# Causal masks by 64-column matmuls, and a stationary padded from 16 to 128 columns

## The chip, the cores and the metric

The kernel runs on one core of one Trainium2 chip. The metric is the device time of one execution in microseconds (us), as the median of the runs shown. Where a profile is read, times are those of one profiled execution.

## The reference, cut to what matters

Two layers, each an attention block and a gated MLP block, on 2048 rows of 640 numbers. Only the attention concerns us. It has 32 heads of 20 columns, and the rows are cut into four segments of 512, inside which each row sees itself and the rows before it:

```python
H = 32; Dh = D // H; N = 4; L = S // N          # D = 640, S = 2048, so L = 512
mask = (ar[:, None] < ar[None, :]) * (-1e9)     # ar = arange(L)
for s in range(N):
    logits = einsum("bhqd,bhkd->bhqk", qs, ks) * scale + mask
    p = softmax(logits, axis=-1)
    a_dot = einsum("bhqk,bhkd->bhqd", p, vs)
    ...                                          # a memory of the segments before, mixed in by a gate
```

## The kernel before, in words

Each layer runs three phases: `phase1a` (attention, class `Attention`), `phase1b` (attention's output matmul for the last rows, layer norm, the MLP's first matmul) and `phase2` (the spatial matmul and the MLP's last matmul). The change touches `phase1a` and the constants built at the start.

**Pairs and steps.** Attention goes through 64 pairs of heads per layer, 4 segments by 16 pairs. The two heads of a pair lie on partitions 0 to 63 and 64 to 127 of one tile `qk`, so that their matmuls use the upper and the lower 64 rows of the array: two instructions with 64 rows each, one per head, follow each other and run side by side. A pair takes three steps c = 0, 1, 2 of `scores` (line 791). A step computes, for pair n, blocks of the transposed logits into the PSUM tile `es` (keys on the partitions, line 816), and for pair n+2 blocks of the logits into the PSUM tile `mp` (queries on the partitions, line 816 too). Steps 0 and 2 have one block of each kind; step 1 has two of each. A block is 128 partitions by 128 to 512 columns, and its one square of 128 by 128 on the diagonal has to be masked.

**The masks.** `mask` (line 781) is called for each block, each head h and each half s = 0, 1: it adds a large negative number above the diagonal by a matmul that accumulates on the block (line 788). The stationary is `big`, 64 rows by 128 columns, with 60000 on a diagonal that picks the 64 output partitions of half s; the moving operand is `maskq` or `maskk`, which holds -60000 where the mask is to be. The 64 partitions of one half need the mask on 64 columns, those of the other half on all 128, so that two of the four mask matmuls of a block (two heads by two halves) have 64 columns and two have 128. In `es` the half s = 0 is the narrow one, in `mp` the half s = 1. The order on PE is: half 0 of all blocks (`es`, then `mp`), then half 1 of all blocks.

**What follows a step.** ScalarE (ACT) takes exp of `es` into `P` (line 825), VectorE (DVE) reduces `mp` to row maxima `mx` (line 832). Both PSUM tiles exist once, so the next step's blocks wait for these readers. After step 2, DVE splits the maxima, scaled and negated, into two f16 parts, `mh`, 128 rows by 16 columns (lines 836, 837). `maxes` (line 851) turns them on PE by a matmul with `mh` as the stationary and an identity of 128 columns as the moving operand, into `mtp` (line 856); ACT copies the 16 rows to `mr` (line 858), and two DMAs from SyncE's queue (SP) put them into rows of `qk` (line 861), from which the maxima enter the logits of `es` two pairs later. `cast` makes f16 high and low parts of `P` on ACT and GpSimd (POOL, lines 847, 848), `pvs` multiplies them with the values on PE (line 875), and `combine` scales and adds on DVE and POOL.

**Fill.** Between the steps PE works on what the next heads and rows need: projections to values, queries and keys (lines 605, 665), the output projection of earlier rows (line 637), the memory (lines 723, 750 to 752).

**What sets the order.** In `phase1a` PE's order is written by hand (`run`, line 910, a list of jobs with due times, under `manual_schedule(engines={PE})`). The order on ACT, DVE, POOL and SP is made when the program is built, by a scheduler that estimates times of all instructions, PE's too. Work with a high priority may be pulled ahead: the first two tiles of `phase1b` (line 316) are loaded and normalized (lines 259, 209, 211, 218) while attention still runs.

Of the kernel before, what the change touches and what calls it, by code (L numbers as in the profile page):

```python
# [8 lines left out]
F32 = mybir.dt.float32  # L9
F32R = mybir.dt.float32r  # L10
F16 = mybir.dt.float16
# [3 lines left out]
ALU = mybir.AluOpType  # L15
# [60 lines left out]
class Weight:  # L76


    def __init__(self, g, nm, c, dram, c0, cols):
        self.g, self.nm, self.c, self.dram, self.c0, self.cols = g, nm, c, dram, c0, cols  # L80
        self.nk = (dram.shape[0] + 127) // 128
        self.kept = [g.nc.dram_tensor(f"w_{nm}{p}", (128, self.nk, cols), F16, kind="Internal").ap() for p in "hl"]
        self.made = False
# [380 lines left out]
def attn_consts(g, cp, beta):  # L464
    nc, tc = g.nc, g.tc

    g.big = cp.tile([128, 192], F16, name="big")
    g.mask = {nm: cp.tile([128, 128], F16, name="mask" + nm) for nm in "qk"}  # L470
    with tc.tile_pool(name="tmp", bufs=1) as tp, tc.tile_pool(name="acp", bufs=1, space=PSUM) as pp:
        f = tp.tile([128, 192], F32, name="fmask")
        for t, n, b, sg, op in ((g.big, 192, -64, 1, ALU.not_equal), (g.mask["q"], 128, 0, -1, ALU.is_ge), (g.mask["k"], 128, -64, 1, ALU.is_ge)):
            nc.vector.memset(f, 0.0)
            for h in range(2):
                v = f[64 * h:64 * h + 64, :n]
                nc.gpsimd.affine_select(v, v, [[sg, n]], op, BIG if op is ALU.not_equal else -BIG, base=b, channel_multiplier=-sg)
            nc.vector.tensor_copy(t, f[:, :n])

        g.gate = cp.tile([128, H], F32, name="gate")  # L480
        g.iomg = cp.tile([128, H], F32, name="iomg")
        nc.sync.dma_start(g.gate, beta.rearrange("(o h) -> o h", o=1).to_broadcast((128, H)))
        nc.scalar.activation(g.iomg, g.gate, AF.Exp)
        nc.vector.tensor_scalar(g.iomg, g.iomg, 1.0, None, ALU.add)
        nc.scalar.activation(g.gate, g.gate, AF.Exp, scale=-1.0)
        nc.vector.tensor_scalar(g.gate, g.gate, 1.0, None, ALU.add)


        row = tp.tile([1, 3, 128], F32, name="mrow")
        nc.vector.memset(row, 0.0)  # L490
        for h in range(2):
            nc.vector.memset(row[:, 0, 64 * h + 62:64 * h + 63], 1.0)
            nc.vector.memset(row[:, 1, 64 * h + 63:64 * h + 64], 1.0)
            nc.vector.memset(row[:, 2, 64 * h + 60:64 * h + 64], MS)
        g.keep = cp.tile([128, 3], F32, name="keep")
        g.qrow = cp.tile([128, 1], F32, name="qrow")
        g.qrow16 = cp.tile([128, 1], F16, name="qrow16")
        kp = pp.tile([128, 4], F32, name="kp")
        for i in range(3):
            nc.tensor.matmul(kp[:, i:i + 1], row[:, i, :], g.ident[0:1, 0:1], start=True, stop=True)  # L500
        nc.vector.tensor_copy(g.keep, kp[:, 0:3])

    g.bmask = cp.tile([128, NU, 8], F32, name="bmask")
    nc.gpsimd.memset(g.bmask, 1.0)
    for m in range(NU):
        n, b = len(TH[m]), 128 * m - DH * TH[m][0]
        v = g.bmask[:, m, :n]
        nc.gpsimd.affine_select(v, v, [[-DH, n]], ALU.is_ge, 0.0, base=b, channel_multiplier=1)
        nc.gpsimd.affine_select(v, v, [[DH, n]], ALU.is_ge, 0.0, base=DH - 1 - b, channel_multiplier=-1)
# [5 lines left out]
class Attention:  # L515
# [9 lines left out]
    def __init__(self, g, x, o_d, x1_d):  # L525
        self.g, self.nc, self.tc = g, g.nc, g.tc
        self.x, self.o_d, self.x1_d = x, o_d, x1_d
        self.st = g.st
        self.gm, self.ot = {}, {}
        self.phq = {}  # L530
        self.P, self.Pf, self.mx, self.mh = {}, {}, {}, {}
        self.pv, self.o = {}, {}
        self.mem, self.last, self.stacked = None, -1, -1
        self.now, self.later, self.rd = None, {}, set()
# [11 lines left out]
    def setup(self, ctx):  # L546
        g, nc, tc = self.g, self.nc, self.tc
        pool = lambda n, b, **k: ctx.enter_context(tc.tile_pool(name=n, bufs=b, reuse_waits="tile", **k))
        sk, self.p3, self.pl2 = pool("ak", 1), pool("a3", 2), pool("al2", 2)
        av, self.u4, self.u2, self.u1 = pool("av", 1), pool("au4", 4), pool("au2", 2), pool("au1", 1)  # L550
        self.e2, self.e1, ax = pool("ae2", 2), pool("ae1", 1), [pool(f"ax{i}", 1) for i in range(2)]
        self.pl1, self.bg = pool("al1", 1), pool("abg", 2)
        self.pd = pool("apd", 2, space=PSUM)
        self.px = pool("apx", 1, space=PSUM)
        self.pm = pool("apm", 1, space=PSUM)
        self.pe = pool("ape", 1, space=PSUM)
        self.po = pool("apo", 1, space=PSUM)
        self.qk = [sk.tile([128, 2, L], F16, name=f"qk{i}") for i in range(self.NQK)]
        self.vs = [p.tile([128, 4, H, 2 * DH + 1], F16, name=f"vs{i}") for i, p in enumerate((av, sk))]
        for t in self.vs:  # L560
            nc.gpsimd.memset(t[:, :, :, DH:DH + 1], 1.0)
        self.xt = [p.tile([128, 2, KD, L], F16, name=f"xt{i}") for i, p in enumerate(ax)]
        self.mst = [self.u1.tile([128, NU, 8, DH + 1], F32, name=f"mst{i}") for i in range(2)]

    def start(self):
# [215 lines left out]
    def mask(self, out, nm, h, o, s):  # L781

        g, nc = self.g, self.nc
        r = slice(64 * h, 64 * h + 64)

        c = slice(64 * s, 128) if nm == "q" else slice(0, 64 * s + 64)
        m = slice(0, 128 - 64 * s) if nm == "q" else slice(64 - 64 * s, 128)
        nc.tensor.matmul(out[:, o + c.start:o + c.stop], g.big[r, 64 - 64 * s:192 - 64 * s], g.mask[nm][r, m], start=False,  # L788
                         stop=s == 1, skip_group_check=True)

    def scores(self, n, c):

        g, nc = self.g, self.nc
        todo = []
        if 0 <= n < self.N:
            q, k = self.qk[n % self.NQK][:, 0], self.qk[n % self.NQK][:, 1]
# [6 lines left out]
        m = n + self.LM  # L803
# [9 lines left out]
        for out, o, w, a, nr, ac, b, bc, _, _ in todo:  # L813
            for h in range(2):
                r = slice(64 * h, 64 * h + nr)
# [12 lines left out]
        if 0 <= m < self.N:  # L828
            if c == 0:
                self.mx[m] = self.pl2.tile([128, 2, 4], F32, tag="mx", name="mx")  # L830
            for i, o, w in red:
                nc.vector.tensor_reduce(self.mx[m][:, :, i], mp[:, :, o:o + w], AX.X, ALU.max)  # L832
            if c == 2:
                mx = self.mx[m]
                mh = self.mh[m] = self.pl2.tile([128, 2, 2, 4], F16, tag="mh", name="mh")
                nc.vector.tensor_scalar(mh[:, :, 0], mx, -1.0 / MS, None, ALU.mult)
                nc.vector.scalar_tensor_tensor(mh[:, :, 1], mx, -1.0 / MS, mh[:, :, 0], ALU.mult, ALU.subtract)

# [12 lines left out]
    def maxes(self, n):  # L851

        g, nc = self.g, self.nc
        del self.mx[n]
        tp = self.pm.tile([128, 512], F32, tag="ms", name="mtp")[:16, :128]
        nc.tensor.matmul(tp, self.mh.pop(n).rearrange("p h i t -> p (h i t)"), g.ident16, start=True, stop=True)
        mr = self.pl2.tile([16, 128], F16, tag="mr", name="mr")
        nc.scalar.copy(mr, tp)
        for h in range(2):
            r = 64 * h + 60  # L860
            nc.sync.dma_start(self.qk[n % self.NQK][r:r + 2, 0].rearrange("i (t c) -> i t c", t=4), mr[8 * h:8 * h + 8])
# [192 lines left out]
def interleaved_layers(ctx, tc, x, wq, wk, wv, wo, beta, w_in, w_sp, b_sp, w_out, out):  # L1054
    nc = tc.nc
    g = Ctx()
    g.nc, g.tc = nc, tc
    cp = consts(g, ctx)
    attn_consts(g, cp, beta)
    prologue(g, ctx, wv, wq, wk, wo, w_in, w_out)  # L1060

# [50 lines left out]
```

## Time and profile before

| | before |
|---|---|
| time, median of 3 runs (lowest to highest) | 2532.6 us (2525.33 to 2532.61) |
| span of the profiled execution | 2529.2 us |
| PE busy in it | 2270.2 us (90%), 21706 matmuls |
| DVE, ACT, POOL busy | 1525.9, 1139.9, 939.6 us |
| masks, line 788 | 4096 matmuls, 98.2 to 1938.5 us |
| turns of the maxima, line 856 | 128 matmuls, 109.7 to 1927.0 us |

The three times are of unprofiled runs. The profiled execution has its span alone, from its first instruction to its last; with whatever lies around the span it stands within the range of the runs, 3.4 us under their median at most.

Attention fills about 100 to 720 us (first layer) and 1338 to 1945 us (second layer) of the span; in between and behind lie the phases without masks. In rows of the timeline the columns are start, duration, engine, line, operation, the program's names, the stationary's and moving operand's shapes ("64\*128 64x64" is a stationary of 64 rows and 128 columns with 64 moving columns on 64 rows), and the number of instructions merged into the row. Matmuls overlap: their durations reach to the end of the array's pipeline, so the pace of a row of matmuls is read from the distance of starts, not from durations. PEld is the loading of the stationary.

### The profile page before, as it was taken

The numbers are of one execution on the slowest core, as the hardware profiler recorded it, in microseconds if no ns is written. First come the engines' busy times: TensorE is split into PE (matmuls) and PEld (weight loads), VectorE is DVE, ScalarE is ACT, GpSimd is POOL, SyncE is SP. The second block draws the span as 40 slices with busy tenths as digits, with TensorE's granted clock in tenths as the row PEclk, the third lists the DMA queues.
The fourth block names the chain that finished last, engine by engine and source line by source line (L and its number), as shares of the span: only waits on it lengthen the run. The fifth ranks groups of instructions, "written<-read, shape, count | busy, mean of one in ns | idle before, by whom it ended". The sixth has DMA issues, their size and how long they took to land. (4 is left out here: it accounts for less than half of the span.)

```text
span 2529.2 us, 52414 instructions
## 1 busy us (share of the span) xinstructions
PE 2270.2 (90%) x21706; PEld 1358.8 (54%) x21706; DVE 1525.9 (60%) x2925; ACT 1139.9 (45%) x1388; POOL 939.6 (37%) x711
## 2 busy tenths in 40 slices
PE   4678788899989998999988889889998999999998
PEld 2345455565655554555554456546565555555555
DVE  6678877777755454544335787787775544444431
ACT  4267766677643231221114677767775332111110
POOL 7066666677631000000042677667775110000000
PEclk9899999899999999999999899989999999999999
DMA  4733644423563478766643244342336335777652
GB/s 141 203 96 101 161 112 112 102 67 105 122 185 94 100 224 217 170 163 156 156 88 91 78 114 97 95 112 70 92 111 167 105 91 143 187 188 174 147 140 64
DMA packets 504575, 325.11 MB, mean 129 GB/s; under 512 B 410576, under 2 KB 445520, under 8 KB 499216
## 3 DMA queue, kind: packets, MB, share of 16 engines
q1 hardware_dynamic: 504336, 321.77, 49.9%
q8 instruction: 169, 2.77, 0.5%
q14 instruction: 70, 0.57, 0.1%
HBM read 148.26 MB, written 85.34 MB: 92 GB/s over the span
## 5 line engine op out<-in xcount | busy, mean ns | idle before, releaser
L848 POOL TENSOR_TENSOR PL<-P,PH 128x1280 f16<-128x1280 f32 x248 | 649.2, 2620 | 319.7 <-ACT PH L847 276.4
L832 DVE TENSOR_REDUCE mx<-mp 128x2 f32<-128x1024 f32 (+3 forms) x512 | 408.8, 820 | 136.8 <-PE mp L788 136.2
L825 ACT ACTIVATE P<-es,sc 128x1024 f32<-128x1024 f32 (+1 forms) x384 | 371.5, 967 | 231.5 <-PE mp L788 184.5
L381 PE MATMUL gp<-zh,wt 128*128 128x432 f16 x2048 | 464.1, 347 | 11.6 <-DMA wt<-wn 11.5
L381 PEld LDWEIGHTS <-wt 128*128 128x128 f16 x3072 | 300.7, 98 | 271.0 <-DMA wt<-wn 12.9
L847 ACT CAST PH<-P 128x1280 f16<-128x1280 f32 x256 | 321.2, 1255 | 8.9 <-PE pv L875 1.4
L300 PEld LDWEIGHTS <-th 128*128 128x128 f16 x1920 | 187.7, 98 | 168.7 <-DMA th<-xnhl 4.1
L381 PE MATMUL gp<-zl,wt 128*128 128x432 f16 x1024 | 271.1, 347 | 0.0
L396 POOL MEMSET un<- 128x64 f16 x32 | 4.8, 151 | 682.1 <-DMA ut<-un 630.8
L816 PEld LDWEIGHTS <-qk 64*128 64x128 f16 (+1 forms) x2048 | 81.6, 96 | 280.5 <-issue 204.9
L212 POOL TENSOR_TENSOR lnrs<-lnve,mhalf 128x1 f32<-128x1 f32 x96 | 58.2, 615 | 440.7 <-DVE lnve L211 433.2
L358 DVE TENSOR_REDUCE am<-wr 128x1 f32<-128x2048 f32 x32 | 73.2, 2286 | 213.1 <-DMA wr<-in_B_w_sp_dram 213.1
L816 PE MATMUL es<-qk 64*128 64x512 f16 (+3 forms) x1024 | 143.1, 313 | 60.2 <-ACT P L825 43.8
L384 ACT ACTIVATE u<-gp,bsp,un 128x864 f32<-128x864 f32 x32 | 34.2, 1068 | 354.8 <-PE gp L381 354.8
L605 PE MATMUL vps<-wvh,xt 128*128 128x320 f16 x640 | 162.5, 324 | 26.5 <-DVE phk L693 8.2
L816 PE MATMUL mp<-qk 60*128 60x512 f16 (+3 forms) x1024 | 141.7, 311 | 47.2 <-DVE mx L832 46.5
L410 PE MATMUL cyp<-wuh,ut 128*128 128x320 f16 (+1 forms) x896 | 164.5, 300 | 11.0 <-DMA ut<-un 10.1
L410 PEld LDWEIGHTS <-ut 128*128 128x128 f16 (+1 forms) x1344 | 131.5, 98 | 67.1 <-DMA ut<-un 12.9
L875 PE MATMUL pv<-vs,PH 128*128 128x41 f16 x2560 | 167.6, 183 | 0.0
L875 PE MATMUL pv<-vs,PL 128*128 128x41 f16 x2560 | 163.9, 181 | 1.6 <-POOL PL L848 1.6
L788 PEld LDWEIGHTS <-big 64*128 64x128 f16 x4096 | 139.1, 97 | 40.7 <-issue 4.7
L368 ACT ACTIVATE wn<-wr,ivw 128x1024 f16<-128x1024 f32 x64 | 71.9, 1143 | 185.5 <-DVE ivw L363 95.3
(186 smaller groups left out, 4331.7 us busy)
## 6 DMA issues: line engine op xcount, KB each, us to landing
wr<-in_B_w_sp_dram SPq DMA_DIRECT2D x32, 1024.0 KB
qk<-st SPq DMA_DIRECT2D x256, 120.0 KB
z<-z SPq DMA_DIRECT2D x32, 432.0 KB
cz<-z SPq DMA_DIRECT2D x32, 432.0 KB
xt<-in_A_x_dram SPq DMA_DIRECT2D x32, 320.0 KB
st<-qhl SPq DMA_DIRECT2D x40, 256.0 KB
st<-khl SPq DMA_DIRECT2D x40, 256.0 KB
x<-x SPq DMA_DIRECT2D x32, 320.0 KB
```

The lines of the kernel that those rows point to most:

```text
L300: nc.tensor.matmul(zp[:, n, :FHH], a[:, k, :], b[:, k, c:c + FHH], start=(k == 0 and j == 0), stop=(k == KD - 1 and j == 2))
L358: nc.vector.tensor_reduce(am, wr, AX.X, ALU.max, apply_absolute_value=True)
L381: nc.tensor.matmul(gp[:, n, :FHH], wt[:, k // 8, a, k % 8, :], b[:, k, n * FHH:(n + 1) * FHH], start=(k == 0 and j == 0), stop=(k == NT - ...
L410: nc.tensor.matmul(yp[:, n, :320], a[:kn[k], k, :], b[:kn[k], k, n * 320:(n + 1) * 320], start=(k == 0 and j == 0), stop=(k == KO - 1 and ...
L605: nc.tensor.matmul(ps, a[:, k, c], b[:, k, n * 320:(n + 1) * 320], start=(i == 0), stop=(i == 14))
L788: nc.tensor.matmul(out[:, o + c.start:o + c.stop], g.big[r, 64 - 64 * s:192 - 64 * s], g.mask[nm][r, m], start=False, stop=s == 1, skip_gr ...
L816: nc.tensor.matmul(out[:, h, o:o + w], a[r, ac], b[r, bc], start=o == 0, stop=False, skip_group_check=True)
L825: nc.scalar.activation(P[:, :, 512 * c:512 * c + ew], es[:, :, :ew], AF.Exp, scale=g.esc)
L832: nc.vector.tensor_reduce(self.mx[m][:, :, i], mp[:, :, o:o + w], AX.X, ALU.max)
L847: nc.scalar.copy(PH, P[:, h])
L848: (nc.gpsimd if h == 0 or n < self.N - self.TAIL else nc.vector).tensor_tensor(PL, P[:, h], PH, ALU.subtract)
L875: nc.tensor.matmul(pv[:, i, h, :], x[:, c:c + 128], v[:, j, h0 + h, :], start=(j == 0 and x is PH), stop=(j == i and x is PL), skip_group_ ...
```

## The change

The roles of the two mask operands are exchanged. The pattern of steps becomes the stationary (`stepq` and `stepk`, 192 columns wide, of which 128 are taken, shifted by 64 for the half), and the diagonal of 60000 becomes the moving operand (`eye`, 64 columns). A matmul now covers all 128 partitions of a strip of 64 columns, where before it covered 64 partitions and up to 128 columns. All four mask matmuls of a block have 64 columns. The number of matmuls, their order and their rows stay.

The stationary `mh` of the turn becomes the first 16 columns of one of two lasting tiles `mhs` of 128 columns, whose other columns are set to zero once per layer. The turn's matmul then writes 128 rows of PSUM instead of 16, of which ACT copies the same 16.

```diff
-    g.big = cp.tile([128, 192], F16, name="big")
-    g.mask = {nm: cp.tile([128, 128], F16, name="mask" + nm) for nm in "qk"}
+    g.eye = cp.tile([128, 64], F16, name="eye")
+    g.step = {nm: cp.tile([128, 192], F16, name="step" + nm) for nm in "qk"}
...
-        for t, n, b, sg, op in ((g.big, 192, -64, 1, ALU.not_equal), (g.mask["q"], 128, 0, -1, ALU.is_ge), (g.mask["k"], 128, -64, 1, ALU.is_ge)):
+        for t, n, b, sg, op in ((g.eye, 64, 0, 1, ALU.not_equal), (g.step["q"], 192, -64, 1, ALU.is_ge), (g.step["k"], 192, 64, -1, ALU.is_ge)):
...
+        self.mhs = [sk.tile([128, 128], F16, name=f"mhs{i}") for i in range(2)]
+        for t in self.mhs:
+            nc.gpsimd.memset(t, 0.0)
...
-        c = slice(64 * s, 128) if nm == "q" else slice(0, 64 * s + 64)
-        m = slice(0, 128 - 64 * s) if nm == "q" else slice(64 - 64 * s, 128)
-        nc.tensor.matmul(out[:, o + c.start:o + c.stop], g.big[r, 64 - 64 * s:192 - 64 * s], g.mask[nm][r, m], start=False,
-                         stop=s == 1, skip_group_check=True)
+        c = o + 64 * s
+        nc.tensor.matmul(out[:, c:c + 64], g.step[nm][r, 64 - 64 * s:192 - 64 * s], g.eye[r], start=False, stop=s == 1,
+                         skip_group_check=True)
...
-                mh = self.mh[m] = self.pl2.tile([128, 2, 2, 4], F16, tag="mh", name="mh")
+                mh = self.mhs[m % 2][:, :16].rearrange("p (h i t) -> p h i t", h=2, i=2)
...
-        tp = self.pm.tile([128, 512], F32, tag="ms", name="mtp")[:16, :128]
-        nc.tensor.matmul(tp, self.mh.pop(n).rearrange("p h i t -> p (h i t)"), g.ident16, start=True, stop=True)
+        tp = self.pm.tile([128, 512], F32, tag="ms", name="mtp")[:, :128]
+        nc.tensor.matmul(tp, self.mhs[n % 2], g.ident16, start=True, stop=True)
...
-        nc.scalar.copy(mr, tp)
+        nc.scalar.copy(mr, tp[:16])
```

PE's order is the same before and after, instruction for instruction; what changes there is operands and widths. On PE, in a step with one block of each kind, the program before has, from the second mask matmul of `es` to the first of its half 1 (`big` is the stationary, a row LDWEIGHTS loads it, the two numbers are the size of what is written):

```order
L788 LDWEIGHTS big
L788 MATMUL es<-maskk,big 128x64
L788 LDWEIGHTS big
L788 MATMUL mp<-maskq,big 128x128
L788 LDWEIGHTS big
L788 MATMUL mp<-maskq,big 128x128
L788 LDWEIGHTS big
L788 MATMUL es<-maskk,big 128x128
```

The same place on PE in the program after (two lines of code are added above the masks in sum, so that line 788 is now 790):

```order
L790 LDWEIGHTS stepk
L790 MATMUL es<-eye,stepk 128x64
L790 LDWEIGHTS stepq
L790 MATMUL mp<-eye,stepq 128x64
L790 LDWEIGHTS stepq
L790 MATMUL mp<-eye,stepq 128x64
L790 LDWEIGHTS stepk
L790 MATMUL es<-eye,stepk 128x64
```

The matmuls stand where they stood; each writes 64 columns, and the stationary differs between `es` and `mp`.

The other engines' order is made anew by the scheduler, which has other estimates for PE. ACT's order is nearly the same; on DVE and SP most rows keep their place or move by a few, and the largest move is that of the first two tiles of `phase1b`. Their statistics (line 209, from the tile `x`, with a number to tell the buffers apart) stand on DVE, before the change, late in attention, at the pairs of the last segment:

```order
L832 TENSOR_REDUCE mx<-mp 128x2
L209 BN_STATS lnst<-x_11881 128x6 x2
L836 TENSOR_SCALAR mh<-mx 128x2x4
L209 BN_STATS lnst<-x_11894 128x6 x2
L210 BN_AGGR lnmv<-lnst 128x2
L837 SCALAR_TENSOR_TENSOR mh<-mx,mh 128x2x4
```

On DVE after the change they stand some 130 instructions earlier, behind the last pair of an earlier segment (`x_11821` and `x_11834` are the same two tiles):

```order
L888 TENSOR_TENSOR rs<-pv,iomg 128x8
L889 RECIPROCAL rs<-rs 128x8
L893 TENSOR_TENSOR ab<-pv,rs 128x328
L209 BN_STATS lnst<-x_11821 128x6 x2
L834 TENSOR_REDUCE mx<-mp 128x2 x2
L209 BN_STATS lnst<-x_11834 128x6
L210 BN_AGGR lnmv<-lnst 128x2
```

The statistics moved ahead past many reductions of `mp`; on SP the two loads of these tiles (line 259) moved ahead by some 70 DMAs with them. The same happens in the second layer.

More of the change, by code (lines that the diff above doesn't have):

```diff
@@ L530, in __init__ @@
         self.phq = {}
-        self.P, self.Pf, self.mx, self.mh = {}, {}, {}, {}
+        self.P, self.Pf, self.mx = {}, {}, {}
         self.pv, self.o = {}, {}
```

## The prediction

> **What bounds the kernel now.** I read first the busy shares, then two stretches of attention (columns: stretch, length, busy time of PE, PEld, DVE, ACT, POOL with counts, granted clock, DMA share, GB/s).
>
> ```profile
> PE 2270.2 (90%) x21706; PEld 1358.8 (54%) x21706; DVE 1525.9 (60%) x2925; ACT 1139.9 (45%) x1388; POOL 939.6 (37%) x711
> ```
>
> ```profile
> 260.00:360.00 100.00, 79.78 (x1073) 52.02 (x1074) 79.61 (x154) 69.87 (x94) 59.70 (x41) 0.93 0.59 149
> 560.00:660.00 100.00, 92.69 (x1359) 58.50 (x1358) 76.82 (x145) 72.55 (x86) 75.18 (x50) 0.95 0.35 96
> ```
>
> The change acts in attention alone, some 1225 us of the span. There PE is the busiest engine late in a layer (92.69 of 100) and level with DVE early (79.78 against 79.61), and the other three work three quarters of the time. So PE leads, but not by much. Next, the waits of PE by releaser (total, times, longest):
>
> ```profile
> PE mp L816 <- DVE mx L832: 46.5, 43, 2.9
> PE es L816 <- ACT P L825: 43.8, 66, 3.6
> PE mtp L856 <- DVE mh L837: 42.9, 22, 6.8
> PE es L816 <- DMA qk<-mr: 13.8, 9, 3.6
> ```
>
> PE waits some 147 us, in 140 pieces of about 1 us. The first two are loops: masks finish `mp` or `es`, the reader empties it, PE may write the next block. A shorter mask lets the reader start sooner, so a gain there passes through the loop if the reader was idle. Last, the chain of waits through the second layer's attention, 1345 to 1945 us:
>
> ```profile
> by line: issue 7.7%; PE kps L665 6.5%; PE qps L665 6.0%; PE pv L875 6.0%; PE es L816 5.3%; PE vps L605 4.8%; ACT P L825 4.7%; DVE mx L832 4.6%; ACT PH L847 4.3%; PE mp L816 4.1%; POOL PL L848 4.0%; PE yps L637 3.3%; PE num L723 2.3%; DMA xt
> ```
>
> PE's entries and "issue" that stand here sum to 46% (7.7 + 6.5 + 6.0 + 6.0 + 5.3 + 4.8 + 4.1 + 3.3 + 2.3). The masks are not among the thirteen, so `es` and `mp` masks have at most 2.3% each, 27.6 us of 600 together.
>
> **The masks.** The pace is read from starts. A step with two blocks of each kind (four instructions per row, two pairs of heads):
>
> ```profile
> 408.07 0.22 PE L788 MATMUL es<-maskk,big 64*128 64x64 f16 x4
> 408.13 0.27 PE L788 MATMUL mp<-maskq,big 64*128 64x128 f16 x4
> 408.24 0.28 PE L788 MATMUL es<-maskk,big 64*128 64x128 f16 x4
> 408.35 0.22 PE L788 MATMUL mp<-maskq,big 64*128 64x64 f16 x4
> 408.51 0.31 PE L637 MATMUL yps<-woh,o 128*128 128x320 f16 x1
> ```
>
> Two pairs of 64 columns take 0.06 us (408.13 − 408.07), two of 128 take 0.11 (408.24 − 408.13, and again 408.35 − 408.24): 0.030 and 0.055 us a pair, so 0.025 saved for each pair that becomes narrow. The last row of masks, 0.16 to the next matmul, is narrow before and after and keeps its price. How many there are:
>
> ```profile
> L788 PE MATMUL es<-maskk,big 64*128 64x128 f16 x1024 | 96.3, 222 | 0.0
> L788 PE MATMUL mp<-maskq,big 64*128 64x128 f16 x1024 | 95.7, 221 | 0.0
> ```
>
> 2048 wide matmuls are 1024 pairs: 1024 × 0.025 = 25.6 us of PE time. Nothing is added: as many matmuls and loads as before, and a stationary of the same 64 rows and 128 columns.
>
> **The turn of the maxima.** With and without the turn between the same neighbours:
>
> ```profile
> 406.03 0.18 PE L875 MATMUL pv<-vs,PL 128*128 128x41 f16 x1
> 406.14 0.22 PE L856 MATMUL mtp<-ident,mh 128*16 128x128 f16 x1
> 406.29 0.31 PE L637 MATMUL yps<-woh,o 128*128 128x320 f16 x1
> ...
> 411.71 0.18 PE L875 MATMUL pv<-vs,PH 128*128 128x41 f16 x1
> 411.73 0.18 PE L875 MATMUL pv<-vs,PL 128*128 128x41 f16 x1
> 411.76 0.30 PE L637 MATMUL yps<-woh,o 128*128 128x320 f16 x1
> ```
>
> Without it `yps` starts 0.03 us after the last `pv`; with it 0.26 (406.29 − 406.03). The 128 columns of the turn are worth 0.055 by the mask pair. So 0.26 − 0.03 − 0.055 = 0.175 us is stall: about 0.08 ahead of the turn and 0.095 behind it. The one thing that sets this matmul apart from its neighbours is its stationary of 16 columns. If all are 128 wide, I expect the array to go through without a seam. 128 turns × 0.175 = 22.4 us; at the 22 that wait for `mh` the 0.08 ahead lies inside the wait, which takes off 1.8: 20.6 us.
>
> The loads of the two stationaries:
>
> ```profile
> L788 PEld LDWEIGHTS <-big x4096: 92/94/148, 98.2 to 1938.5; 64*128 64x128 f16 x196
> L856 PEld LDWEIGHTS <-mh x128: 85/85/89, 109.7 to 1927.0; 128*16 128x16 f16 x128
> ```
>
> The narrow load takes 85 ns, a wide one 94: padding lengthens the load by 9 ns, 1.2 us over 128, at most, and hidden where it is pulled ahead. The bounds of this term are −1.2 us (the stall has another cause) and +22.4. I take 20.6, since both neighbours of the turn show the seam only there. [...]
>
> **What else moves.** The zeroing of `mhs` is two POOL instructions per layer ahead of the first pairs; the nearest row is a zeroing of half the columns:
>
> ```profile
> L396 POOL MEMSET un<- 128x64 f16 x32 | 4.8, 151 | 682.1 <-DMA ut<-un 630.8
> ```
>
> At twice 151 ns each, 4 × 0.3 = 1.2 us in all if nothing covered them; they stand where PE still waits for weights and rows, so I cost them at 0. ACT still copies 16 rows. The early statistics on DVE are the one move that could matter. Before, the two loads are issued and DVE waits:
>
> ```profile
> 678.15 0.87 SPq L259 DMA_DIRECT2D x<-x  x2
> ...
> 681.16 0.89 DVE L209 BATCH_NORM_STATS2 lnst<-x 128x6 f32<-128x320 f32 x2 [4.93 <-DMA x<-x]
> ```
>
> DVE stands 4.93 us for a load that takes 3 us from issue (681.16 − 678.15); the `mx` reductions are queued behind it, and PE's `mp` behind these. After, the same wait comes earlier in the layer. It may be 0 or again about 5 us, so −5 to +5 per layer, ±10 in all; I take 0, since the same two loads stand ahead of the same kind of work. The other small moves on DVE and SP I hold to be inside that.
>
> **The sum.** PE gets 25.6 + 20.6 = 46.2 us of work less. What of it reaches the end is what lies on the chain. For the masks at most 27.6 of the layer's 512 × 0.030 + 512 × 0.055 = 43.5 us: 63%. For PE as a whole at least 46%. Between these I take 55%: 25 us. It is the most that can go while the other engines' pieces stay: when the chain's PE pieces shrink, chains over DVE and ACT that are now a little shorter come last instead. The gain per wait, 46 us over 140, is 0.33 us against waits of 1 us, so PE stays bound to the same partners. I take four fifths of it, 20 us; this last factor is a choice. 2529.2 − 20 = 2509.2 us of span. The profiled execution lies 3.4 us under the median at most; set on the median, 2532.6 − 20 = 2512.6, rounded to 2513.
>
> **The rivals.** *Both edits act, half of it arrives* (forecast): 2505 to 2520, chance 0.54.
>
> *Only the masks gain*: the seam at the turn is due to its place (operands from DVE just before) and not to its width. Then 25.6 × 0.55 × 0.8 = 11 us, 2521. Against it: after the turn there is no such operand and still 0.095 us are lost. 0.14.
>
> *The waits take it*: DVE's `mx`, ACT's `P` and DVE's `mh` already end 133 us of PE's waits; early in a layer DVE is as busy as PE. If these readers are full rather than released late, PE's 46 us turn into longer waits, and at most 6 arrive: about 2528. For it: 79.61 on DVE; against it: 92.69 on PE late in the layer. 0.17.
>
> *All of it arrives*, because masks stand ahead of the readers in both loops: 2532.6 − 46 = 2486. The 27.6 us bound speaks against it. 0.08.
>
> *Loading sets the pace* (the slower side): in long runs of narrow masks the columns no longer cover the loads. Rows of one load and one matmul of 41 columns start 0.025 us apart (411.71, 411.73, 411.76). If the loads of two heads can't run side by side, each pair needs two, 0.05 us; 2048 pairs then take 102.4 us instead of 1024 × (0.030 + 0.055) = 87.0, 15.4 more, the padded load adds up to 1.2, and if the turn's seam is a load that isn't covered either, nothing is gained there: at the chain's 55% to all of it, 9 to 17 us slower, about 2545. It decides from 0.0425 us a narrow pair on, where masks gain nothing. The row at 408.07 has two narrow pairs in succession at 0.030 and loads for the next just behind them; after the change runs of eight follow each other, where a load made early counts less. 0.07. [...]
>
> **How the numbers follow.** About 0.3%, 7.6 us, is what a measurement of this kernel can tell from no change. Faster by more: nearly all of the forecast (0.52 of 0.54), most of the masks-only case (0.12), all of the full gain (0.08), a quarter of the waits case (0.04): 0.76. Slower: most of the last rival, 0.06. Same: 0.18. The range holds the forecast, the masks-only case, the waits case and the mild part of the full gain: 2495 to 2530. It leaves out the slower case and the larger full gains, and the ±10 of the moved statistics lie inside it.
>
> **What would show it.** In the profile after: all mask rows 64x64, in a step with four blocks eight pairs in about 0.24 us plus the end, pairs still 0.03 apart; `mtp` with a stationary of 128 columns, 0.03 behind `pv` and the next matmul about 0.055 behind it; PE's busy time down, and PE's waits for `mx`, `P` and `mh` up by half of what PE saved. The prediction is wrong on masks if late pairs of a run start 0.04 or more apart, wrong on the turn if 0.1 stays on either side, wrong on the share if the waits grow by nearly 46 or not at all, and wrong on the moved statistics if DVE stands over 5 us ahead of them.

## The result, and the profile after

The changed kernel takes 2521.4 us, the median of 20 runs (2513.47 to 2527.63), against 2534.6 for the kernel before (20 runs). The ratio is 0.9943, with a 95% interval of 0.9931 to 0.9956: 14.4 us faster, where 20 were forecast. The profiled execution after has a span of 2520.5 us and a time of 2522.2 us, so 1.7 us lie around the span.

Both savings on PE are there. First the timeline of PE, in a step with two blocks of each kind and in a step with one (start, duration, engine, line, operation, names, shapes, instructions in the row):

```profile
404.93 0.22 PE L790 MATMUL es<-eye,stepk 64*128 64x64 f16 x4
404.99 0.22 PE L790 MATMUL mp<-eye,stepq 64*128 64x64 f16 x4
405.05 0.22 PE L790 MATMUL es<-eye,stepk 64*128 64x64 f16 x4
405.11 0.22 PE L790 MATMUL mp<-eye,stepq 64*128 64x64 f16 x4
405.26 0.31 PE L640 MATMUL yps<-woh,o 128*128 128x320 f16 x1
...
407.89 0.19 PE L790 MATMUL es<-eye,stepk 64*128 64x64 f16 x2
407.92 0.19 PE L790 MATMUL mp<-eye,stepq 64*128 64x64 f16 x2
407.95 0.19 PE L790 MATMUL es<-eye,stepk 64*128 64x64 f16 x2
407.98 0.19 PE L790 MATMUL mp<-eye,stepq 64*128 64x64 f16 x2
408.10 0.19 PE L877 MATMUL pv<-vs,PH 128*128 128x41 f16 x1
```

All pairs start 0.03 us apart, to the end of a run of eight. The larger step takes 0.33 us to the next matmul, where the prediction's row took 0.44 (408.51 − 408.07): 0.11 for four narrowed pairs. Next, a turn of the maxima, again behind a `pv`, and here with a projection behind it:

```profile
380.33 0.18 PE L877 MATMUL pv<-vs,PL 128*128 128x41 f16 x1
380.36 0.22 PE L858 MATMUL mtp<-ident,mhs 128*128 128x128 f16 x1
380.41 0.38 PE L668 MATMUL qps<-xt,wqh 128*128 128x512 f16 x1
```

0.03 ahead and 0.05 behind, where it was 0.11 and 0.15. The seam is gone. By starts over the whole trace, the masks save about 28 us of PE's work (1024 pairs that started 0.055 us apart now start 0.028 apart, as medians) and the turns about 22 (0.185 us × 128, less 2 us at turns that wait anyway): 50 us, of which 14 arrived. Where the rest went shows in two places. The first is PE's waits (total, times, longest):

```profile
PE mtp L858 <- DVE mhs L839: 56.0, 23, 7.5
PE mp L818 <- DVE mx L834: 54.3, 49, 4.2
PE es L818 <- ACT P L827: 48.9, 70, 2.7
...
PE es L818 <- DMA qk<-mr: 7.3, 3, 4.0
```

The three that were 133 us are 159; the largest growth, 13 us, is at the turn. The second is the busy line:

```profile
PE 2237.1 (89%) x21706; PEld 1332.5 (53%) x21706; DVE 1555.7 (62%) x2925; ACT 1137.3 (45%) x1388; POOL 945.9 (38%) x715
```

DVE is busy 29.8 us longer (1525.9 before) with the same 2925 instructions. The groups of DVE say which (total busy time, then mean ns of one); first before:

```profile
L691 DVE TENSOR_SCALAR eq<-eq,sc 128x512 f32<-128x512 f32 x60 | 55.0, 916 | 0.0
...
L836 DVE TENSOR_SCALAR mh<-mx 128x8 f16<-128x8 f32 x128 | 40.1, 313 | 2.7
L588 DVE TENSOR_SCALAR xt<-xt,lnmv,lnrs 128x640 f32<-128x640 f32 x32 | 27.6, 868 | 4.4 <-POOL lnrs L212 3.9
```

and after:

```profile
L694 DVE TENSOR_SCALAR eq<-eq,sc 128x512 f32<-128x512 f32 x60 | 61.5, 1024 | 0.0
L838 DVE TENSOR_SCALAR mhs<-mx 128x8 f16<-128x8 f32 x128 | 53.0, 414 | 2.7
...
L591 DVE TENSOR_SCALAR xt<-xt,lnmv,lnrs 128x640 f32<-128x640 f32 x32 | 43.9, 1375 | 6.5 <-POOL lnrs L212 6.3
```

An instruction that scales 8 numbers per partition has a mean of 414 ns. A mean hides two populations, so the next view is that of single lines after (shortest, median and longest of one in ns):

```profile
L838 DVE TENSOR_SCALAR mhs<-mx x128: 154/172/2603, 108.9 to 1916.7; 128x8 f16<-128x8 f32 x128
L591 DVE TENSOR_SCALAR xt<-xt,lnmv,lnrs x32: 592/613/2901, 19.7 to 1685.4; 128x640 f32<-128x640 f32 x32
L834 DVE TENSOR_REDUCE mx<-mp x512: 407/800/1228, 100.4 to 1916.0; 128x2 f32<-128x1024 f32 x43, 128x2 f32<-128x512 f32 x43, 128x2 f32<-128x256 f32 x43, 128x2 f32<-128x768 f32 x42
```

Most `mhs` instructions take about 172 ns, and 8 of the 128 take over 2000. The reductions, which read PSUM, differ by at most 62 ns within a size: the 128 of 1024 columns, 103 of them beside a `PL` on POOL, all take 1208 to 1228 ns. The timeline of all engines shows what happens at one long one:

```profile
174.47 2.62 POOL L850 TENSOR_TENSOR PL<-P,PH 128x1280 f16<-128x1280 f32 x1
...
174.54 2.90 DVE L591 TENSOR_SCALAR xt<-xt,lnmv,lnrs 128x640 f32<-128x640 f32 x1 [0.56 <-POOL lnrs L212]
...
177.36 1.21 DVE L834 TENSOR_REDUCE mx<-mp 128x2 f32<-128x1024 f32 x1
...
178.63 0.34 PE L818 MATMUL mp<-qk 60*128 60x384 f16 x2 [2.42 <-DVE mx L834]
```

DVE's 0.61 us of scaling `xt` begins 0.07 us after POOL's `PL`, and lasts until 177.44, 0.35 us after POOL ends (177.09). The `mx` reduction is queued behind it, and PE waits 2.42 us for that. I call this a hold, and measure it as the time of a DVE instruction above the fast end (the tenth percentile) of the same instruction, where that is over 0.25 us: 106 us in all before, 145 after. Each of the 101 and 135 held instructions overlaps one of POOL, and 95 and 132 us of the held time overlap a `PL`. In this trace `mhs` and `xt`, which work from SBUF to SBUF by tensor_scalar, take up to 2603 and 2901 ns, and no reduction of `mp`, in PSUM, takes over 1228. Nor is every instruction from SBUF to SBUF held: of the 128 reciprocals `rs` (line 889) 81 overlap a `PL`, and none takes over 205 ns. What lets POOL hold DVE is not shown.

### The profile page after: what moved, and what is told of

The parts are those of the page before. It is cut to its first block, busy times and chain, and to the rows that moved or that the text cites. A ratio compares the mean times of both kernels' runs of the same rounds, so it can differ in the third digit from the quotient of the medians.

```text
span 2520.5 us, 52420 instructions
## 1 busy us (share of the span) xinstructions
PE 2237.1 (89%) x21706; PEld 1332.5 (53%) x21706; DVE 1555.7 (62%) x2925; ACT 1137.3 (45%) x1388; POOL 945.9 (38%) x715
## 5 line engine op out<-in xcount | busy, mean ns | idle before, releaser
L410 PEld LDWEIGHTS <-ut 128*128 128x128 f16 (+1 forms) x1344 | 132.3, 99 | 65.7 <-DMA ut<-un 10.2
L300 PE MATMUL zp<-wi1h,th 128*128 128x432 f16 x640 | 149.1, 348 | 4.1 <-DMA th<-xnhl 3.5
```

Of the source, the lines that this page charges most:

```text
L300: nc.tensor.matmul(zp[:, n, :FHH], a[:, k, :], b[:, k, c:c + FHH], start=(k == 0 and j == 0), stop=(k == KD - 1 and j == 2))
L410: nc.tensor.matmul(yp[:, n, :320], a[:kn[k], k, :], b[:kn[k], k, n * 320:(n + 1) * 320], start=(k == 0 and j == 0), stop=(k == KO - 1 and ...
```

## The experiments

Twelve kernels were run in three groups of four; ratios are to the kernel before in the same group (2533.6, 2535.6, 2528.6 us).

**mask_only.** The masks are changed, the turn keeps its 16 columns and its tile. The edit against the changed kernel, cut to the turn:

```diff
-                mh = self.mhs[m % 2][:, :16].rearrange(...)
+                mh = self.mh[m] = self.pl2.tile([128, 2, 2, 4], F16, tag="mh", name="mh")
...
-        nc.tensor.matmul(tp, self.mhs[n % 2], g.ident16, start=True, stop=True)
+        nc.tensor.matmul(tp, self.mh.pop(n).rearrange("p h i t -> p (h i t)"), g.ident16, start=True, stop=True)
```

> The masks of 64 columns alone; the turn of the maxima keeps its 16-column stationary. PE saves 26 us of mask time and nothing at the turn. Theory A (DVE is held by POOL: in the traces a DVE instruction that works from SBUF to SBUF and meets a running subtraction PL on POOL ends only when that ends; these holds sum to 106 us before the change and 145 us after, and the 39 us more gave back part of the gain): if the holds stay near 106 us, 55% of 26 us arrive, 14 us less than before, ratio 0.994 to 0.995, as much as the whole change brought. Theory B (the loops over mp and es pass on only three tenths of what PE saves, whatever the holds are): 8 us less, ratio about 0.997.

2503.8 us, 0.9889 (0.9869 to 0.9908): 28 us faster, as much as the masks save on PE, 14 us better than the whole change, and twice what theory A expected. The run is not PE's saving alone: the scheduler made a new order here too, in which another instruction stands at 316 of DVE's 2925 places, and the holds sum to 120 us.

**pad_only.** The turn is padded, the masks stay: the two `mhs` edits of the change and their zeroing, none of the mask edits.

> The padded stationary of the turn alone; the masks keep their widths. PE saves the seams, about 21 us, and the next matmul starts 0.055 us behind the turn. The two lasting tiles move the memory of other tiles, so the early statistics of the next phase move ahead on DVE here too. Theory A: the holds grow over 106 us with this order, and the gain is small, 0 to 5 us, ratio 0.998 to 1.000. Theory B: three tenths of 21 us, 6 us, ratio 0.9975, whatever the holds are; the gains of the two halves sum to the 14 us of the whole.

2531.2 us, 0.9993 (0.9979 to 1.0008): no difference, as theory A expected, though the seams are gone here too. DVE is busy 1548.4 us, 22.5 more than before, about what PE saves.

**before_pl_in_four** and **change_pl_in_four.** POOL's `PL` is cut in four, in the kernel before and in the changed one.

```diff
-        (nc.gpsimd if h == 0 or n < self.N - self.TAIL else nc.vector).tensor_tensor(PL, P[:, h], PH, ALU.subtract)
+        if h == 0 or n < self.N - self.TAIL:
+            for i in range(0, 1280, 320):
+                nc.gpsimd.tensor_tensor(PL[:, i:i + 320], P[:, h, i:i + 320], PH[:, i:i + 320], ALU.subtract)
+        else:
+            nc.vector.tensor_tensor(PL, P[:, h], PH, ALU.subtract)
```

> The kernel before with POOL's subtraction PL cut into four in the same way. Theory A: holds fall from 106 to under 45 us, 5 to 15 us less time than before, ratio 0.994 to 0.998; and the changed kernel cut in four lies 20 us or more under this one, since what gave back its gain is gone. Theory B: ratio 0.998 to 1.003, and the distance to the changed kernel cut in four is the 14 us of the change as it stands.

> The changed kernel with POOL's subtraction PL (1280 columns, 2.6 us) cut into four of 320 columns, same numbers. POOL does the same work with 744 more instructions. Theory A: a DVE instruction that meets one waits for a quarter of the length, the holds fall from 145 to under 60 us, DVE's mh and the mx behind it come sooner, PE's wait for mh falls from 56 to under 35 us, and the time falls to 25 to 35 us under the kernel before, ratio 0.986 to 0.990. Theory B: the loops pass on no more than now; holds fall or not, ratio stays 0.994, or rises where POOL's additional instructions make it late.

2490.5 us, 0.9832 (0.9809 to 0.9855), and 2458.8 us, 0.9715 (0.9691 to 0.9739): 43 and 72 us faster than before. The second has the shortest time of all kernels. Both gained more than either theory expected, while the holds, 64 and 95 us, fell less than theory A expected: against the kernels with a whole `PL` they fell by 43 and 50 us, and the time by 43 and 58. The group of `PL` on POOL before, and cut in four:

```profile
L848 POOL TENSOR_TENSOR PL<-P,PH 128x1280 f16<-128x1280 f32 x248 | 649.2, 2620 | 319.7 <-ACT PH L847 276.4 <-ACT mr L858 17.8 <-PE mp L788 14.9
```

```profile
L850 POOL TENSOR_TENSOR PL<-P,PH 128x320 f16<-128x320 f32 x992 | 778.5, 818 | 202.3 <-ACT PH L847 181.9 <-PE mp L788 5.2 <-POOL PL L850 4.4
```

The cut costs POOL 129 us more work, 0.17 us for each of 744 further instructions, and still gains. The line of the first part of `mh` in the kernel before (shortest, median, longest, ns):

```profile
L836 DVE TENSOR_SCALAR mh<-mx x128: 154/172/2566, 109.3 to 1925.4; 128x8 f16<-128x8 f32 x128
```

The same line in before_pl_in_four, and then that kernel's busy line:

```profile
L836 DVE TENSOR_SCALAR mh<-mx x128: 154/186/1350, 108.6 to 1879.2; 128x8 f16<-128x8 f32 x128
```

```profile
PE 2264.1 (91%) x21706; PEld 1358.5 (55%) x21706; DVE 1484.8 (60%) x2925; ACT 1137.9 (46%) x1388; POOL 1060.6 (43%) x1455
```

The longest hold of this line is halved, and DVE is busy 41 us less with the same instructions: about what the time fell by, without any work taken off PE. PE's wait at the turn falls from 42.9 to 19.4 us:

```profile
PE mtp L860 <- DVE mh L837: 19.4, 16, 4.7
```

**mask_only_shifted.** As mask_only, but two zeroed tiles of 128 columns that nobody reads stand in the pool where the change has `mhs`.

```diff
+        for t in [sk.tile([128, 128], F16, name=f"mhs{i}") for i in range(2)]:
+            nc.gpsimd.memset(t, 0.0)
```

> The masks of 64 columns alone, with two tiles of the size of the padded ones allocated and zeroed in attention's pool and not used. DVE, ACT and POOL have instruction for instruction the order of the changed kernel; the turn keeps its 16 columns and its seam. Theory C: the 14 us that the early statistics cost are lost here too, 8 to 14 us under before, ratio 0.994 to 0.997, with about 15 us of holds in the last segments. Theory D: like the masks alone, 28 us under before, ratio 0.989.

2517.7 us, 0.9927 (0.9909 to 0.9945): 10 us of mask_only's gain are lost to tiles that nobody reads, fewer than theory C expected. They change the order of the program: ACT, DVE and POOL now have the order of the changed kernel, instruction for instruction, with the early statistics. PE's waits for `mh`, in mask_only and here:

```profile
PE mtp L855 <- DVE mh L836: 35.0, 16, 7.7
```

```profile
PE mtp L857 <- DVE mh L838: 51.4, 20, 7.3
```

The last segment of each layer shows where it may come from (stretch from the first to the last turn of the segment, length, busy time of PE, PEld, DVE, ACT, POOL with counts), in mask_only and then here:

```profile
565.60:687.10 121.50, 109.66 (x1670) 70.50 (x1668) 95.70 (x192) 89.46 (x107) 91.30 (x62) 0.94 0.47 122
1780.80:1902.00 121.20, 108.96 (x1673) 70.93 (x1669) 96.39 (x192) 89.61 (x107) 93.03 (x62) 0.96 0.50 136
```

```profile
568.30:694.50 126.20, 109.77 (x1672) 70.56 (x1669) 100.83 (x192) 89.68 (x107) 92.61 (x62) 0.95 0.46 118
1780.50:1907.20 126.70, 109.31 (x1672) 70.94 (x1669) 99.81 (x192) 89.72 (x107) 91.88 (x62) 0.95 0.50 137
```

With 192 instructions in all four rows, DVE is busy 5.1 and 3.4 us longer, and the segments last 4.7 and 5.5 us longer. These 10.2 us are as much as the ratios differ by (0.0038 of 2535 us); in the two profiled executions other stretches gave half of it back (spans of 2503.8 and 2509.1 us).

**mhs_in_constants.** The whole change, but `mhs` stands among the constants, so that the pool is as before. The edit against the changed kernel (the zeroing moves along):

```diff
+    g.mhs = [cp.tile([128, 128], F16, name=f"mhs{i}") for i in range(2)]
...
-        self.mhs = [sk.tile([128, 128], F16, name=f"mhs{i}") for i in range(2)]
+        self.mhs = g.mhs
```

> The whole change, with the two padded tiles among the constants that are allocated once ahead of both layers, instead of in attention's own pool. Work and PE order are those of the changed kernel; the statistics of the next phase's first tiles stand late on DVE again, as before the change. Theory C (the padded tiles push other tiles' memory; with that the first tile of the next phase is free earlier, the scheduler pulls its statistics ahead and shifts DVE's order in the last segment by eight, and there DVE meets POOL's subtractions: holds of 14.9 us in the last segment of each layer against 6.6 and 6.9 before, which cost the 14 us between masks alone and the whole): holds in the last segments back to 6 or 7 us, time 28 us (masks alone) plus 10 to 20 us (turn) under before, ratio 0.981 to 0.985. Theory D (the padded turn itself costs: 128 rows written instead of 16, or lasting tiles instead of rotating ones): no better than the changed kernel, ratio 0.993 to 0.996.

2511.8 us, 0.9906 (0.9888 to 0.9923): better than the change, by 9 us, but no better than mask_only and short of what was expected. The statistics are late again (672 us instead of 592), yet DVE's busy time is still 1552.0 us: its holds moved to other places. So the placement, with its order, is one part of the loss, and not all.

**constants_and_pl_in_four.** Both of these edits together.

> The whole change, padded tiles among the constants, and POOL's subtraction cut into four. Theory C: in the changed kernel cut in four the last segments already lost little (117.9 and 121.7 us against 123.3 and 120.5 in the kernel before cut in four), so 0 to 10 us less than that kernel, ratio 0.967 to 0.972, below all others. Theory D: the same as the changed kernel cut in four, ratio 0.9715.

2466.3 us, 0.9731 (0.9712 to 0.9749), not separated from change_pl_in_four: with `PL` in short pieces, no effect of the placement of `mhs` can be told.

**masks_all_wide.** In the kernel before, all masks have 128 columns; the added ones add zeros.

```diff
-    g.mask = {nm: cp.tile([128, 128], F16, name="mask" + nm) for nm in "qk"}
+    g.mask = {nm: cp.tile([128, 192], F16, name="mask" + nm) for nm in "qk"}
...
-        c = slice(64 * s, 128) if nm == "q" else slice(0, 64 * s + 64)
-        m = slice(0, 128 - 64 * s) if nm == "q" else slice(64 - 64 * s, 128)
+        c = slice(0, 128)
+        m = slice(64 - 64 * s, 192 - 64 * s)
```

> The kernel before with all mask matmuls 128 columns wide (the additional columns add zeros): 1024 pairs go from 0.031 to 0.055 us, 25 us more PE time; the statistics stay late. It shows what PE time is worth in the other direction. If PE's time lies on the chain by 55% as the prediction put it: 14 us slower, ratio 1.0055. If nearly all of PE's time counts, as the masks alone gave 28 us for 26 to 28 saved: 25 us slower, ratio 1.010. Theory B (loops pass on three tenths): 8 us, ratio 1.003.

2524.5 us, 0.9954 (0.9936 to 0.9971): 12 us faster with 28 us more work on PE (by starts, as a pair goes from 0.028 to 0.055 us; 25 were expected). The scheduler made another order, for PE's new estimates or for the two wider constants, and in it the second part of `mh` is hardly ever held. Its line before, and here:

```profile
L837 DVE SCALAR_TENSOR_TENSOR mh<-mx,mh x128: 111/168/2581, 109.5 to 1925.6; 128x8 f16<-128x8 f32 x128
```

```profile
L837 DVE SCALAR_TENSOR_TENSOR mh<-mx,mh x128: 113/168/491, 109.5 to 1918.0; 128x8 f16<-128x8 f32 x128
```

Its DVE is busy 1495.1 us, 30.8 less than before, and its mean granted clock is 0.970 against 0.958, as medians of the group's runs. As a measure of what PE work is worth the run is spoilt by that; of all the expectations it is the clearest miss, since none allowed for a new order.

**change_mx_in_psum, before_mx_in_psum, change_four_and_psum.** `mx` is put into unused columns of the PSUM bank of `pv`, so that the `mh` instructions no longer read it from SBUF; in the changed kernel, in the one before, and in the changed one with `PL` in four.

```diff
+        self.pvt = self.po.tile([128, 512], F32, name="pvt")
...
-                self.mx[m] = self.pl2.tile([128, 2, 4], F32, tag="mx", name="mx")
+                self.mx[m] = self.pvt[:, 384 + 8 * (m % 2):392 + 8 * (m % 2)].rearrange("p (h t) -> p h t", h=2)
...
-            self.pv[n] = self.po.tile([128, 512], F32, tag="pv", name="pv")[:, :8 * 41].rearrange(
+            self.pv[n] = self.pvt[:, :8 * 41].rearrange(
```

> The changed kernel with the row maxima mx kept in PSUM, in unused columns of the bank that holds pv, instead of SBUF; the two small instructions that make mh then read PSUM. In the traces no DVE instruction that reads PSUM is held by POOL. Theory A (time follows PE work and the holds of DVE by POOL, both about one to one): the holds of mh, 54 us of 145, are gone, PE's wait for mh falls from 56 to under 30 us, and the time is 45 to 65 us under before, ratio 0.974 to 0.982. Rival (the holds only go along; time is set by the loops over mp and es): ratio 0.993 to 0.996 with PE's wait for mx and P grown by what the wait for mh lost.

> The kernel before with mx in PSUM in the same way. Theory A: 43 us of 106 us of holds gone, 30 to 43 us less, ratio 0.983 to 0.988; the changed kernel with mx in PSUM lies 25 us or more under this one, since the holds that grew with the change were mostly those of mh. Rival: ratio 0.998 to 1.002, distance 14 us.

> The changed kernel with both: PL cut into four and mx in PSUM. Theory A: of its 95 us of holds some 58 (mh) go, so 90 to 125 us under before, ratio 0.951 to 0.965, below all others. Rival: as with PL in four alone, ratio 0.9715.

2927.8 us (1.1574, 1.1551 to 1.1597), 2978.7 us (1.1764, 1.1731 to 1.1797) and 2902.9 us (1.1475, 1.1452 to 1.1499). As tests of time all three are void: `pv` and the maxima now share a tile, and PE's matmuls into `pv` wait for DVE. PE's waits in change_mx_in_psum:

```profile
PE pvt L878 <- DVE mhs L840: 205.9, 122, 3.8
PE pvt L878 <- DVE pvt L835: 192.1, 118, 4.4
```

What they do show is the hold itself. The line of the first part of `mhs` there:

```profile
L839 DVE TENSOR_SCALAR mhs<-pvt x128: 151/166/168, 108.7 to 2318.2; 128x8 f16<-128x8 f32 x128
```

With its input in PSUM, none of the 128 took over 168 ns, where the longest was 2603. That rests on few meetings: only 4 of the 128 began while a `PL` ran, against 25 in the changed kernel, and these 4 took at most 166 ns.

**mask_only_pl_in_four.** mask_only and the cut `PL`.

> Masks of 64 columns alone, turn with its 16 columns, PL cut into four. It shows what the padded turn is worth where holds are short. If the seam's 21 us of PE count one to one: about 50 us under before, 20 over the changed kernel cut in four, ratio 0.979 to 0.982. If the turn brings nothing because mh comes late in any case: like the changed kernel cut in four, ratio 0.971 to 0.974.

2469.1 us, 0.9758 (0.9738 to 0.9778), against 0.9715 (0.9691 to 0.9739) with the padded turn added: with `PL` cut, padding brings some 11 us of its 22, between the two expectations, and the intervals just touch.

**The ledger.** In microseconds, to the kernel before: PE's work by starts, DVE's busy time (its instructions are the same everywhere here), their sum, and the measured time.

| kernel | PE work | DVE busy | sum | measured |
|---|---|---|---|---|
| change | −50 | +30 | −20 | −14 |
| mask_only | −28 | +9 | −19 | −28 |
| pad_only | −22 | +23 | +1 | −2 |
| mask_only_shifted | −28 | +24 | −4 | −18 |
| mhs_in_constants | −50 | +26 | −24 | −24 |
| masks_all_wide | +28 | −31 | −3 | −12 |
| before_pl_in_four | 0 | −41 | −41 | −43 |
| mask_only_pl_in_four | −28 | −22 | −50 | −61 |
| constants_and_pl_in_four | −50 | −11 | −61 | −68 |
| change_pl_in_four | −50 | −10 | −60 | −72 |

The sum orders most of the kernels and hits within 15 us. It is a fit and not a law: a hold may cost nothing where PE does not wait behind it, which no run separates. It also leaves out the granted clock, which moves with the holds. Its median over the runs is 0.954 to 0.959 in the six kernels with 106 us of holds or more, the one before among them, and 0.968 to 0.971 in the five with less than 100. By an estimate, 0.012 of 2530 us is up to 30 us of PE's time, and no run separates what came by the clock from what came by the holds themselves. PE's saving alone does not order them: 50 us saved gave 14 and 24, and none saved gave 43.

## Why the prediction was right in sign and range, and where it was off

- **The masks**, 25.6 us of PE: right, about 28 by starts. The rival that loads set the pace has fallen: runs of eight pairs keep 0.03 us.
- **The turn**, 20.6 us: right as to PE, about 22. The narrow stationary makes the seam: in pad_only, where the masks stay, the turn's start is also 0.025 us behind `pv` and 0.055 ahead of the next matmul, as medians, against 0.110 and 0.155 before.
- **The share that arrives**, 55% and then four fifths "a choice": the step that failed. PE's pieces on the chain were read as the share of a saving that arrives, and one share was used for both edits. mask_only saves 28 on PE and is 28 faster, though its DVE is busy 9 us longer; pad_only saves 22 and gains nothing; the change saves 50 and gains 14. What share would arrive with the order of the other engines kept is not shown in general.
- **The moved statistics**, costed at 0 "since the same two loads stand ahead of the same kind of work": wrong. I looked for DVE standing idle ahead of them, and that wait even became shorter (4.93 and 4.10 us before). The rows after:

```profile
592.11 0.89 DVE L209 BATCH_NORM_STATS2 lnst<-x 128x6 f32<-128x320 f32 x2 [1.79 <-DMA x<-x]
...
1810.42 0.89 DVE L209 BATCH_NORM_STATS2 lnst<-x 128x6 f32<-128x320 f32 x2 [1.53 <-DMA x<-x]
```

  The cost is not in that wait but, as far as the runs show, in holds: 109 us of them overlap POOL's `PL` in mask_only and 123 in mask_only_shifted. These two runs price the placement with its new order at 10 us, the end of the ±10 that the prediction gave.
- **The holds**: the term that is missing from the sum. The profile before shows them (an `mh` that takes 154 to 2566 ns), and the prediction used DVE's busy shares without asking why equal instructions differ. They grew from 106 to 145 us, and DVE's busy time by 30. The early statistics are not all of it: in mask_only these stay late (666 us), and the holds grow to 120 all the same. If the masks' full arrival is taken as the share, the share and the holds were wrong in opposite directions, so that 20 came near 14 is in part luck.
- **The rivals.** The result has the figure of "only the masks gain", 2521, and padding did gain nothing in time, but not by that rival's mechanism: the seam went. "The waits take it" describes part of it: PE's three waits grew by 26 us, half of the saving, as the prediction's test asked. But the readers were not full; they were held.

What stays open: why padding the turn gains nothing while `PL` is long. mask_only_shifted and the change have the same order on DVE, ACT and POOL and differ by the seam's 22 us on PE, and their times agree (0.9927 and 0.9943, intervals overlapping). In the change, the busy time of DVE is 5.9 us higher and PE's three waits are 15 us longer (159.2 against 144.4). An earlier turn may bring other DVE instructions under a `PL`, but no run isolates that. The scheduler also makes a new order with the cut `PL`, so its 43 us are the worth of shorter pieces and of the new order together.

## What to carry to other kernels

Price a change of a scheduled kernel twice: by the work it removes, and by what the new order does to instructions that another engine holds (DVE's beside POOL's: 106 us before, 145 after); even an unused tile in a pool can make a new order. Equal instructions with very unequal durations (here 154 to 2603 ns), and an engine's busy time that changes at an equal count, are where to look in the profile. Where a long POOL instruction holds DVE on the path, cut it into short ones: here that, with the new order it made, was worth 43 us, three times the change itself.

## What the hardware showed beside

One hold may cost more than itself. The windows of the changed kernel around the hold shown above (stretch, length, busy time of PE with count, granted clock, DMA share, GB/s):

```profile
171.00:174.40 3.40, 2.85 (x56) 1.00 0.36 122
174.40:177.80 3.40, 1.81 (x24) 1.00 0.00 0
177.80:181.20 3.40, 2.16 (x24) 0.67 0.20 66
181.20:184.60 3.40, 3.33 (x35) 0.50 0.40 130
```

PE waits in the second window and into the third, and from 178.93 to 185.76 us, when it has work again, its clock is granted at half; in the 3.41 us ahead of that, as long as 19 of this trace's stretches at half clock, PE was busy for 0.99. In this trace that is the pattern: ahead of each of the 36 falls of the clock behind the first 100 us, PE was busy for at most 62% of the 3.41 us before, against 89% over the span. So the falls stand behind PE's waits, though not every wait has one. The mean granted clock, as the median over the runs, was 0.959 before, 0.955 after, 0.971 in change_pl_in_four and 0.969 in before_pl_in_four. So part of what shorter pieces gain may come by way of the clock; how much was not separated.

A small stationary among wide ones was not cheap here: a turn with 16 columns cost 0.185 us more than one with 128, although its load is 10 ns shorter (85 against 95).
